# Frequency 32 as a member of frequency 0's group: four groups a block instead of five, in a fused convolution and spectral-filter kernel

## The chip, the cores and the metric

The kernel runs on one core of a Trainium2 chip. A core has a matrix engine (PE, its weight loads shown as PEld), a vector engine (DVE), an activation engine (ACT), GpSimd (POOL) and a queue engine (SP). SP, ACT and POOL also issue transfers, which sixteen DMA engines carry out. The metric is the device time of one execution in microseconds (us); what is compared is the median of several runs. The profile is one execution with its own span.

## The reference, cut to what matters

```python
x = A_u                                            # (1, 2048, 640)
g = sigmoid((x * gate_w).sum(-1, keepdims=True))
# a: long convolution over time, one kernel K[d, l] per channel, by FFT of length 4096
y = irfft(rfft(x^T, 4096) * rfft(K, 4096), 4096)[:, :, :2048]
a = y^T + x * D_skip
# b: 2-D real FFT over time and channel, times a complex weight, and back
b = irfft2(rfft2(x) * (w_r + 1j * w_i), s=(2048, 640))
out = g * a + (1 - g) * b
```

The kernel K is itself computed (`K = 2 Re sum_n C exp(A dt l)`). Only the convolution's inverse and the last sum are touched by the change.

## The kernel before, in words

The 640 channels are worked on in four blocks of 160 (`c` = 0 to 3). A transform of length 4096 is split in two: 33 outer frequencies k = 0 to 32, each with an inner transform of 64 points as a matrix product with a table of its own (`T.w2` forward, `T.w3` back), and an outer real transform of 32 points (tables `T.e1` forward; `T.e3`, `T.e3e` back). `POS_K` orders the frequencies: first the sixteen odd ones, then the even ones 0, 2, ... 32, so frequency 0 stands at place `K0` = 16 and frequency 32 at place 32, alone behind two sets of sixteen. A frequency has a real and an imaginary outer part, 64 rows each. Frequencies 0 and 32 are real on the outer side, so each of them needs only one half of such a pair.

Earlier phases make the transforms of the input (`u_d` in DRAM), the filtered half b (`s3e_d`) and the kernel K (`k_d`). The change lies in `phase_d` alone, the last stage, about 177 us long. For each block it does, in groups of four pairs of frequencies:

- `load`: fetch the group's part of `u_d` into the tile `us` (L782, issued on ACT's queue).
- `fronts`: PE multiplies by `w2` (helper line L348, tile `p_s`); DVE and POOL form the complex product with `us` (L795, L796, L800, L801) into `t2`. Two pairs make one half of a group.
- `backs`: PE multiplies `t2` by `w3` (L814, tile `p_i`); ACT copies the result into `s3` (L816; two buffers) and stores it in `s3_d` (L823), 640 KB a group. `backs` of a group runs behind the `fronts` of a later one: the list `late` holds two groups back, near the end one.

Beside this main stream, `merge` mixes in three others by weights written by hand:

- `first`: the forward outer transform of the next block's K (L335 with ACT copies L336), ten pieces a block.
- `last_e(c, a)`: the outer inverse of half b, in two calls a block (L160, tile `p_e`, then DVE L875 into `oe`).
- `last_c(c, a)`: the outer inverse of the convolution of block c, in two calls (L892, tile `p_c`, DVE L897, then a sum with `oe`, and the store of `out`). It reads the tile `t3`, which `load_c` fetches from `s3_d` on SP's queue in two loads of 1280 KB (L865), each when the stores of its rows have landed.

Frequency 32 is a fifth group of its own: half a pair on 64 partitions, with two matmuls in `fronts` and two in `backs`, a copy of 128x160 (L818) and a store of 40 KB (L820) to row 33 of `s3_d`. Row 33 is the row of frequency 0's unused half, which group 8's store has written before, so L820 waits on ACT until that store has landed.

A block thus has five steps g (for c = 3 the small group comes fourth). `last_e(c)` runs at g = 1 and 2 (for c = 0 at 2 and 3); `load_c(c-1)` at g = 1 and 2; `last_c(c-1)` at g = 3 and 4 for c = 1 and 2. For c = 3, `load_c(3)` begins at g = 2 and 3, and both calls of `last_c(2)` stand behind the last group, before `last_c(3)`. What stands in each engine's program is a static order that the framework derives from the code's order, tile buffers and its own estimate of times; each engine takes its instructions in that order.

Of the kernel before, what the change touches and what calls it, by code (L numbers as in the profile page):

```python
# [765 lines left out]
def phase_d(tc, A, T, ctx, out):  # L766
    nc = tc.nc
# [16 lines left out]
    def fronts(c, g0, gn, st):  # L784
        nl, us = st.nl, st.us
        nj = nl // 64

        t2 = st.t2 = wk.tile([128, 8, 160], F32, tag="t2", name="t2")
        for h in range(0, gn, 2):
            hn = min(2, gn - h)  # L790
            pv, _ = stage2(nc, ps, T.w2, T.t1[c], g0 + h, hn)
            uu = us[:nl, h:h + hn]
            ma = wk.tile([128, 2, 2, 160], F32, tag="ma", name="ma")
            mb = wk.tile([128, 2, 2, 160], F32, tag="mb", name="mb")
            V.tensor_tensor(out=ma[:nl, :hn], in0=pv, in1=uu, op=ALU.mult)  # L795
            V.tensor_tensor(out=mb[:nl, :hn], in0=pv, in1=uu[:, :, ::-1, :], op=ALU.mult)  # L796
            for j in range(nj):
                l = slice(64 * j, 64 * j + 64)
                o = slice(nj * h + j, nj * (h + hn), nj)
                (G if j else V).tensor_tensor(out=t2[0:64, o, :], in0=ma[l, :hn, 0, :], in1=ma[l, :hn, 1, :], op=ALU.subtract)  # L800
                (V if j else G).tensor_tensor(out=t2[64:128, o, :], in0=mb[l, :hn, 0, :], in1=mb[l, :hn, 1, :], op=ALU.add)  # L801
            yield 0.55 * hn

    def backs(c, g0, gn, st):
        t2 = st.t2
        s3 = w2k.tile([128, 8 if gn > 1 else 1, 160], F32, tag="s3%d" % min(2, gn), name="s3")
        np_ = gn * st.nl // 64
        k0 = 2 * g0
        for h in range(0, np_, 4):
            hn = min(4, np_ - h)  # L810
            p = ps.tile([128, 2, 512], F32, tag="ps", name="p_i2")
            for i in range(hn):
                for x in (0, 64):
                    T.mm = P.matmul(p[x:x + 64, i // 2, 160 * (i % 2):160 * (i % 2) + 160], T.w3[:, k0 + h + i, x:x + 64], t2[:, h + i, :], start=True, stop=True)  # L814
            if hn == 4:
                S.copy(s3[:, h:h + 4, :].rearrange("p (x y) d -> p x (y d)", x=2), p[:, :, 0:320])  # L816
            else:
                S.copy(s3[:, h, :], p[:, 0, 0:160])  # L818
            if k0 == 32:
                nc.scalar.dma_start(T.s3_d[c, 33], s3[0:64, 0, :])  # L820
            elif h or (c, g0) == (3, 12):
                x = h if (c, g0) == (3, 12) else 0
                T.sd = nc.scalar.dma_start(T.s3_d[c, 2 * (k0 + x):2 * (k0 + h) + 8].rearrange("(x k) a d -> (k a) x d", k=2), s3[:, x:h + 4, :])  # L823
            yield 0.27 * hn

    groups = [(c, g0, min(4, 17 - g0)) for c in range(4) for g0 in ((0, 4, 8, 12, 16), (0, 4, 8, 16, 12))[c == 3]]
    late, sts, t3s, t3es, oes = [], {}, {}, {}, {}

    def mains(i):
# [7 lines left out]
        while len(late) > (1 if i > 15 else 2):  # L837
# [111 lines left out]
    run(last_c(2, 0))  # L949
# [27 lines left out]
```

## Time and profile before

| | |
|---|---|
| runs | 617.16 us median of 3 (616.8 to 620.78) |
| profiled execution | 616.28 us, of which span 614.5 us |
| last stage | from about 437.8 us to the end of the span |
| DMA in the whole span | 101.98 MB |
| small stores (L820) | 4, 40 KB each |
| copies of 128x160 on ACT (L818) | 4, 0.29 us each |

How to read it: the timeline lists instructions by start and busy time, with the idle time of the engine ahead of them in brackets and what ended it. In the timeline and the chain an fp32 matmul shows as two records, so x16 is eight matmuls. "issue" means that the profile shows nothing that the engine waited for; a wait for a transfer can hide there. A stage's table gives each engine's busy time, the clock granted to PE and the busy share of the DMA engines.

### The profile page before, as it was taken

The numbers are of one execution on the slowest core, as the hardware profiler recorded it, in microseconds if no ns is written. First come the engines' busy times: TensorE is split into PE (matmuls) and PEld (weight loads), VectorE is DVE, ScalarE is ACT, GpSimd is POOL, SyncE is SP. The second block draws the span as 40 slices with busy tenths as digits, with TensorE's granted clock in tenths as the row PEclk, the third lists the DMA queues.
The fourth block names the chain that finished last, engine by engine and source line by source line (L and its number), as shares of the span: only waits on it lengthen the run. The fifth ranks groups of instructions, "written<-read, shape, count | busy, mean of one in ns | idle before, by whom it ended". The sixth has DMA issues, their size and how long they took to land.

```text
span 614.5 us, 16646 instructions
## 1 busy us (share of the span) xinstructions
PE 539.0 (88%) x7084; PEld 411.1 (67%) x7084; DVE 500.0 (81%) x748; ACT 364.6 (59%) x659; POOL 267.2 (43%) x246
## 2 busy tenths in 40 slices
PE   9688989989968989989799989898989979998864
PEld 6576667766746666766667766566878768787731
DVE  6961697598899988999999999978496975987863
ACT  4556675677847777897599897798523213231210
POOL 4921261152527344455326334345243546565450
PEclk9899989989979987999799999999989989999987
DMA  8787204154512411243242122115967989799985
GB/s 340 304 290 248 70 25 167 30 200 153 215 44 65 138 44 54 66 137 109 65 139 69 36 87 89 49 45 183 349 228 264 259 264 325 230 298 288 260 217 195
DMA packets 47987, 101.98 MB, mean 166 GB/s; under 512 B 3220, under 2 KB 32680, under 8 KB 46152
## 3 DMA queue, kind: packets, MB, share of 16 engines
q1 hardware_dynamic: 24792, 67.74, 34.0%
q10 hardware_dynamic: 20080, 22.52, 11.8%
q0 software_dynamic: 3040, 10.65, 5.3%
q8 instruction: 56, 0.92, 0.6%
q14 instruction: 19, 0.16, 0.1%
HBM read 60.91 MB, written 39.98 MB: 164 GB/s over the span
## 4 chain that ended last, share of the span: by engine, by line
PE 49%; DVE 26%; DMA 9%; ACT 9%; issue 4%; POOL 1%; ACTq 0%; SPq 0%; DVEq 0%; POOLq 0%
PE p_eo L551 8%; PE p_s L335 7%; PE p_s L348 7%; PE p_e L638 5%; PE p_k L693 4%; DMA s_d<-s 3%; PE p_i L814 3%; DVE q L652 2%; PE p_c L892 2%; PE p_p L649 2%; PE p_d L518 2%; PE p_i L565 2%; PE p_t L502 2%; DVE ma L795 2%; PE p_d L519 2%
## 5 line engine op out<-in xcount | busy, mean ns | idle before, releaser
L679 POOL TENSOR_TENSOR y<-e,sc 128x512 f32<-128x512 f32 x40 | 56.7, 1417 | 131.3 <-ACT sc L665 71.9
L348 PE MATMUL p_s<-t,w 128*64 128x160 f32 x1056 | 94.4, 317 | 10.3 <-ACT ut L382 4.5
L348 PEld LDWEIGHTS p_s<-t,w 128*64 128x64 f32 x1056 | 78.0, 140 | 21.2 <-ACT ut L382 5.4
L640 ACT ACTIVATE e<-p_e 128x512 f32<-128x512 f32 x120 | 68.6, 601 | 22.8 <-PE p_e L638 20.4
L551 PE MATMUL p_eo<-td,pmt 107*128 107x321 f32 x204 | 69.0, 458 | 3.9 <-ACT pmt L505 3.9
L693 PE MATMUL p_k<-x,y 128*32 128x64 f32 x2560 | 63.7, 229 | 9.9 <-DVE x L677 2.9
L693 PEld LDWEIGHTS p_k<-x,y 128*32 128x32 f32 x2560 | 46.1, 113 | 38.2 <-issue 29.4
L336 ACT COPY t<-p_s 128x512 f32<-128x512 f32 x40 | 24.5, 621 | 74.0 <-PE p_s L335 54.1
L652 DVE SCALAR_TENSOR_TENSOR q<-q,p_p 128x512 f32<-128x512 f32 x80 | 53.4, 681 | 13.5 <-ACT q L651 11.7
L638 PE MATMUL p_e<-rm,par 128*128 128x512 f32 x120 | 58.8, 520 | 3.4 <-ACT e L640 2.8
L680 POOL TENSOR_TENSOR y<-e,sc 128x512 f32<-128x512 f32 x40 | 54.4, 1359 | 6.5 <-ACT sc L666 6.5
L800 POOL TENSOR_TENSOR t<-ma 64x320 f32<-64x320 f32 x32 | 28.3, 883 | 60.5 <-DVE ma L795 50.8
L551 PEld LDWEIGHTS p_eo<-td,pmt 107*128 107x128 f32 x204 | 38.4, 198 | 19.5 <-ACT pmt L505 6.9
L677 DVE TENSOR_TENSOR x<-e,cx 128x1024 f32<-128x1024 f32 x40 | 48.5, 1213 | 2.2 <-ACT cx L668 2.2
L651 ACT ACTIVATE q<-p_p 128x512 f32<-128x512 f32 x80 | 46.5, 592 | 4.3 <-PE p_p L649 3.8
L335 PEld LDWEIGHTS p_s<-c,kt 128*64 128x64 f32 x640 | 41.2, 141 | 11.5 <-issue 6.7
L335 PE MATMUL p_s<-c,kt 128*64 128x128 f32 x640 | 45.2, 281 | 3.9 <-DVE mb L796 2.0
L814 PE MATMUL p_i<-t,w 128*64 128x160 f32 x528 | 45.0, 305 | 3.6 <-POOL t L801 2.8
L649 PE MATMUL p_p<-rp,par 128*128 128x512 f32 x80 | 43.3, 547 | 4.5 <-DVE q L652 4.4
L795 DVE TENSOR_TENSOR ma<-p_s,us 128x640 f32<-128x640 f32 (+1 forms) x36 | 28.2, 783 | 19.9 <-PE p_s L348 12.5
L814 PEld LDWEIGHTS p_i<-t,w 128*64 128x64 f32 x528 | 38.8, 139 | 8.0 <-POOL t L801 3.4
L816 ACT COPY s<-p_i 128x640 f32<-128x640 f32 x32 | 21.8, 693 | 37.6 <-PE p_i L814 28.5
(153 smaller groups left out, 1190.6 us busy)
## 6 DMA issues: line engine op xcount, KB each, us to landing
u_d<-ut SPq DMA_DIRECT2D x32, 320.0 KB, 2.7
us<-u_d ACTq DMA_DIRECT2D x16, 640.0 KB, 6.4
s_d<-s ACTq DMA_DIRECT2D x15, 640.0 KB, 8.6
t<-s_d SPq DMA_DIRECT2D x6, 1280.0 KB, 10.0
ww<-in_w_l SPq DMA_DIRECT2D x8, 642.0 KB, 4.0
ue<-u_d SPq DMA_DIRECT2D x8, 640.0 KB, 4.4
k_d<-kt SPq DMA_DIRECT2D x4, 1280.0 KB, 7.7
kt<-k_d SPq DMA_DIRECT2D x8, 640.0 KB, 9.2
```

Of the source, the lines that this page charges most:

```text
L335: nc.tensor.matmul(p[64 * ri:64 * ri + 64, j, :], src(i + j), e1[ri], start=True, stop=True)
L348: ins = nc.tensor.matmul(p[64 * j:64 * j + 64, i, 160 * ri:160 * ri + 160], w2[:, x, 64 * ri:64 * ri + 64], t1[:, x // 2 if x < 32 else K0 ...
L551: P.matmul(p[:, :E], st.pmt[:DC, c, w, j, :], tv[:DC, w, c, :], start=c == 0, stop=c == 2)
L638: P.matmul(p[:, :], pars[t], rm[:, c:c + 512], start=True, stop=True)
L640: st.exp = S.activation(ef[:, c:c + 512], p[:, :], AF.Exp)
L649: P.matmul(p[:, :], pars[t], rp[:, c:c + 512], start=True, stop=True)
L652: V.scalar_tensor_tensor(out=qf[:, c:c + 512], in0=qf[:, c:c + 512], scalar=MAGIC, in1=p[:, :], op0=ALU.subtract, op1=ALU.subtract)
L677: V.tensor_tensor(out=x[:, 0].rearrange("p d (h j) -> p d h j", h=2), in0=e[:, :, 0:64].rearrange("p d (h j) -> p d h j", h=2), in1=cx.uns ...
L679: G.tensor_tensor(out=y[:, 1], in0=e[:, :, 64:96], in1=sc[:, 0], op=ALU.mult)
L680: G.tensor_tensor(out=y[:, 0], in0=e[:, :, 64:96], in1=sc[:, 1], op=ALU.mult)
L693: P.matmul(st.pb[32 * r:32 * r + 32, o, :], y[:, ri, 4 * qq + JR[r], :], x[:, ri, 4 * qq + JR[r], :], start=t % 2 + qq + 1 - ri == 0, stop ...
L814: T.mm = P.matmul(p[x:x + 64, i // 2, 160 * (i % 2):160 * (i % 2) + 160], T.w3[:, k0 + h + i, x:x + 64], t2[:, h + i, :], start=True, stop ...
```

## The change

Frequency 32 joins the group that begins at pair 8, the group of frequency 0. In `fronts` that group has a third, smaller part, with its own small tile `u1` and transfer. `t2` has nine columns, and the ninth holds frequency 32. In `backs`, the 64-row matmul that would compute the unused half of frequency 0 takes frequency 32's table and column instead, so its result lands in the right row of the same PSUM bank and goes out with the group's copy and store. A block has four groups; the fifth group's matmuls in `backs`, its copy and its store are gone. The other streams are placed anew: `last_e` at g = 1 and 2 in every block, `last_c(c-1, 0)` at g = 3, `last_c(c-2, 8)` at g = 0 of the block after, `last_c(2, 0)` at g = 3 of the last block, three pieces of `first` a step instead of two, and `late` shrinks to one from step 13.

```diff
-    def load(c, g0, gn, st):
-        nl = st.nl = 128 if g0 < 16 else 64
+    def load(c, g0, st):
         st.us = up.tile([128, 4, 2, 160], F32, tag="us", name="us")
-        nc.scalar.dma_start(st.us[:nl, 0:gn], T.u_d[c, :nl, g0:g0 + gn])
+        nc.scalar.dma_start(st.us[:, :], T.u_d[c, :, g0:g0 + 4])
+        if g0 == 8:
+            st.u1 = w2k.tile([64, 1, 2, 160], F32, tag="u1", name="u1")
+            nc.scalar.dma_start(st.u1[:, :], T.u_d[c, 0:64, 16:17])
...
-        t2 = st.t2 = wk.tile([128, 8, 160], F32, tag="t2", name="t2")
-        for h in range(0, gn, 2):
-            hn = min(2, gn - h)
-            pv, _ = stage2(nc, ps, T.w2, T.t1[c], g0 + h, hn)
-            uu = us[:nl, h:h + hn]
+        t2 = st.t2 = wk.tile([128, 9, 160], F32, tag="t2", name="t2")
+        for h in (0, 2, 4)[:3 if g0 == 8 else 2]:
+            hn, nl = (2, 128) if h < 4 else (1, 64)
+            nj = nl // 64
+            pv, _ = stage2(nc, ps, T.w2, T.t1[c], g0 + h if h < 4 else 16, hn)
+            uu = st.us[:, h:h + 2] if h < 4 else st.u1
...
-        for h in range(0, np_, 4):
-            hn = min(4, np_ - h)
+        for h in (0, 4):
             p = ps.tile([128, 2, 512], F32, tag="ps", name="p_i2")
-            for i in range(hn):
+            for i in range(4):
                 for x in (0, 64):
-                    T.mm = P.matmul(p[x:x + 64, i // 2, 160 * (i % 2):160 * (i % 2) + 160], T.w3[:, k0 + h + i, x:x + 64], t2[:, h + i, :], start=True, stop=True)
-            if hn == 4:
-                S.copy(s3[:, h:h + 4, :].rearrange("p (x y) d -> p x (y d)", x=2), p[:, :, 0:320])
-            else:
-                S.copy(s3[:, h, :], p[:, 0, 0:160])
-            if k0 == 32:
-                nc.scalar.dma_start(T.s3_d[c, 33], s3[0:64, 0, :])
-            elif h or (c, g0) == (3, 12):
+
+                    k, y, o = (32, 0, 8) if x and k0 + h + i == K0 else (k0 + h + i, x, h + i)
+                    T.mm = P.matmul(p[x:x + 64, i // 2, 160 * (i % 2):160 * (i % 2) + 160], T.w3[:, k, y:y + 64], t2[:, o, :], start=True, stop=True)
+            S.copy(s3[:, h:h + 4, :].rearrange("p (x y) d -> p x (y d)", x=2), p[:, :, 0:320])
+            if h or (c, g0) == (3, 12):
...
-    groups = [(c, g0, min(4, 17 - g0)) for c in range(4) for g0 in ((0, 4, 8, 12, 16), (0, 4, 8, 16, 12))[c == 3]]
+    groups = [(c, g0) for c in range(4) for g0 in (0, 4, 8, 12)]
...
-        while len(late) > (1 if i > 15 else 2):
+        while len(late) > (1 if i > 12 else 2):
...
-        for g in range(5):
+        for g in range(4):
             beside = []
-            if g - (c == 0) in (1, 2):
-                beside = [last_e(c, AG * (g - 1 - (c == 0)))]
-            if c and g == 1:
-                load_c(c - 1, 0, 32)
-            if c and g == 2:
-                load_c(c - 1, 32, 32)
-            if c in (1, 2) and g > 2:
-                beside += [last_c(c - 1, AG * (g - 3))]
-            if g == 4 and c < 3:
+            if g in (1, 2):
+                beside = [last_e(c, AG * (g - 1))]
+            if c and g in (1, 2):
+                load_c(c - 1, 32 * (g - 1), 32)
+            if c and g == 3:
+                beside = [last_c(c - 1, 0)]
+            if c > 1 and g == 0:
+                beside = [last_c(c - 2, AG)]
+            if g == 3 and c < 3:
                 load_e(c + 1)
-            if c == 3 and g in (2, 3):
+            if c == 3 and g > 1:
                 load_c(3, 16 * (g - 2), 16)
...
-            streams = [(4.8, mains(5 * c + g))]
+            streams = [(4.8, mains(4 * c + g))]
...
-                streams.append((2.1, some(fst, 2 if g < 4 else 9)))
+                streams.append((2.1, some(fst, 3 if g < 3 else 9)))
...
     load_c(3, 48, 16, 2)
-    run(last_c(2, 0))
     run(last_c(2, AG))
```

Three places of the engines' order, before and changed. The first is PE in block 1, at the end of the step g = 1 (`p_s` with `kt` is a piece of `first`). Before:

```order
L335 MATMUL p_s_6089<-c_65,kt 64x128 x7
L814 MATMUL p_i_6100<-t_5897,w_5268 64x160 [waits Activation_49,Pool_49]
L814 MATMUL p_i_6100<-t_5897,w_5268 64x160
L160 MATMUL p_e<-t3e,c_65 64x320 [waits DVE_49]
L160 MATMUL p_e<-t3e,c_65 64x320
```

Changed:

```order
L335 MATMUL p_s_6078<-c_65,kt 64x128 x7
L815 MATMUL p_i_6089<-t_5859,w_5268 64x160 [waits Activation_49,Pool_49]
L815 MATMUL p_i_6089<-t_5859,w_5268 64x160 x7
L160 MATMUL p_e<-t3e,c_65 64x320 [waits DVE_49]
L160 MATMUL p_e<-t3e,c_65 64x320
L815 MATMUL p_i_6103<-t_5859,w_5268 64x160 [waits DVE_49,PE_49]
L815 MATMUL p_i_6103<-t_5859,w_5268 64x160 x7
```

Before, the two matmuls of `backs(0, 16)` stand here, and `backs(0, 12)` stood at g = 0; now the sixteen of `backs(0, 12)` stand here.

The second is the end of PE's program. Before, `backs(3, 12)` ends, and then both calls of `last_c(2)` follow (`t_6854` is block 2's `t3`):

```order
L814 MATMUL p_i_7097<-t_7044,w_5268 64x160 [waits DVE_49]
L814 MATMUL p_i_7097<-t_7044,w_5268 64x160 x5
L892 MATMUL p_c<-t_6854,c_65 64x480 [waits DMAHW7_49,DMAHW5_49]
L892 MATMUL p_c<-t_6854,c_65 64x480 x3
L892 MATMUL p_c<-t_6854,c_65 64x320 [waits DVE_49]
```

Changed (`p_i_7062` is `backs(3, 8)`, `p_i_7074` and `p_i_7085` are `backs(3, 12)`, `t_6817` is block 2's `t3`):

```order
L815 MATMUL p_i_7062<-t_6920,w_5268 64x160 [waits DVE_49,PE_49]
L815 MATMUL p_i_7062<-t_6920,w_5268 64x160 x2
L888 MATMUL p_c<-t_6817,c_65 64x480 [waits DMAHW6_49,DMAHW3_49]
L888 MATMUL p_c<-t_6817,c_65 64x480 x3
L815 MATMUL p_i_7062<-t_6920,w_5268 64x160 x2
L888 MATMUL p_c<-t_6817,c_65 64x320 [waits DVE_49]
L888 MATMUL p_c<-t_6817,c_65 64x320
L815 MATMUL p_i_7062<-t_6920,w_5268 64x160 x3
L815 MATMUL p_i_7074<-t_7000,w_5268 64x160 [waits Activation_49,Pool_49]
L815 MATMUL p_i_7074<-t_7000,w_5268 64x160 x7
L815 MATMUL p_i_7085<-t_7000,w_5268 64x160 [waits DVE_49,Pool_49]
```

`last_c(2, 0)` with its wait for two loads now stands ahead of all of `backs(3, 12)`. On DVE its first product likewise stands ahead of the last two products of `fronts(3, 12)`, where nothing stood before:

```order
L796 TENSOR_TENSOR ma<-p_s_7024,us 128x640 [waits PE_49,Pool_49]
L797 TENSOR_TENSOR mb<-p_s_7024,us 128x640 [waits Pool_49]
L893 TENSOR_TENSOR ot<-p_c,gate 128x480 [waits DMASW5_49,PE_49]
L801 TENSOR_TENSOR t_7000<-ma 64x2x160 [waits DVE_49]
L802 TENSOR_TENSOR t_7000<-mb 64x2x160 [waits DVE_49]
```

The third is the end of ACT's program. Before:

```order
L816 COPY s_7085<-p_i_7086 128x640 [waits DMAHW0_49,PE_49]
L820 DMA s_d<-s_7079 64x160 [waits DMAHW1_49,Activation_49]
L823 DMA s_d<-s_7085 128x4x160 [waits DMAHW4_49,Activation_49]
L816 COPY s_7085<-p_i_7097 128x640 [waits PE_49]
L823 DMA s_d<-s_7085 128x4x160 [waits DMAHW5_49,Activation_49]
```

Changed:

```order
L816 COPY s_7073<-p_i_7074 128x640 [waits DMAHW4_49,PE_49]
L816 COPY s_7073<-p_i_7085 128x640 [waits PE_49]
L819 DMA s_d<-s_7073 128x4x160 [waits Activation_49] x2
```

The small store with its wait is gone, and both halves of the last group's store now follow the second copy.

More of the change, by code (lines that the diff above doesn't have):

```diff
@@ L777, in phase_d, with fronts @@
     pd = ctx.enter_context(tc.tile_pool(name="d_ps", reuse_waits="tile", bufs=2, space=PSUM))
-    def load(c, g0, gn, st):
-        nl = st.nl = 128 if g0 < 16 else 64
+    def load(c, g0, st):
         st.us = up.tile([128, 4, 2, 160], F32, tag="us", name="us")
-        nc.scalar.dma_start(st.us[:nl, 0:gn], T.u_d[c, :nl, g0:g0 + gn])
-    def fronts(c, g0, gn, st):
-        nl, us = st.nl, st.us
-        nj = nl // 64
-        t2 = st.t2 = wk.tile([128, 8, 160], F32, tag="t2", name="t2")
-        for h in range(0, gn, 2):
-            hn = min(2, gn - h)
-            pv, _ = stage2(nc, ps, T.w2, T.t1[c], g0 + h, hn)
-            uu = us[:nl, h:h + hn]
+        nc.scalar.dma_start(st.us[:, :], T.u_d[c, :, g0:g0 + 4])
+        if g0 == 8:
+            st.u1 = w2k.tile([64, 1, 2, 160], F32, tag="u1", name="u1")
+            nc.scalar.dma_start(st.u1[:, :], T.u_d[c, 0:64, 16:17])
+    def fronts(c, g0, st):
+        t2 = st.t2 = wk.tile([128, 9, 160], F32, tag="t2", name="t2")
[4 more added lines that the diff above has]
+            uu = st.us[:, h:h + 2] if h < 4 else st.u1
             ma = wk.tile([128, 2, 2, 160], F32, tag="ma", name="ma")
             mb = wk.tile([128, 2, 2, 160], F32, tag="mb", name="mb")
-            V.tensor_tensor(out=ma[:nl, :hn], in0=pv, in1=uu, op=ALU.mult)
+            V.tensor_tensor(out=ma[:nl, :hn], in0=pv, in1=uu[:, :], op=ALU.mult)
             V.tensor_tensor(out=mb[:nl, :hn], in0=pv, in1=uu[:, :, ::-1, :], op=ALU.mult)
```

9 lines of the change are left out of this document (4 added, 5 removed).

## The prediction

> **What bounds the kernel now.** I read the page first, for the span, and then a table of the last stage cut at the starts of its blocks, since the change lies there alone.
>
> ```profile
> span 614.5 us, 16646 instructions
> ```
>
> ```profile
> core 0: us, PE busy (x) PEld busy (x) DVE busy (x) ACT busy (x) POOL busy (x), PEclk, DMA share, GB/s
> 437.80:472.30 34.50, 31.80 (x412) 28.53 (x412) 29.36 (x41) 10.73 (x17) 15.47 (x17) 0.95 0.75 270
> 472.30:516.50 44.20, 38.64 (x472) 32.80 (x472) 32.80 (x47) 11.74 (x19) 22.05 (x23) 0.96 0.93 278
> 516.50:556.10 39.60, 36.90 (x472) 31.41 (x472) 33.28 (x48) 11.76 (x19) 23.43 (x25) 1.00 0.93 277
> 556.10:590.70 34.60, 28.27 (x324) 22.89 (x326) 29.60 (x42) 6.67 (x11) 16.86 (x19) 0.97 1.01 273
> 590.70:614.50 23.80, 13.00 (x50) 3.70 (x48) 9.58 (x23) 0.69 (x1) 5.73 (x5) 0.79 0.64 195
> ```
>
> Blocks 0, 1 and 2 are PE's: it is busy 31.80 of 34.50, 38.64 of 44.20 and 36.90 of 39.60 us. In block 3 PE has 6 us free and DVE, busy 29.60 of 34.60, sets the pace. The DMA engines are busy throughout, so a transfer lands long after its issue. The fifth row is the tail: store, load, `last_c(3)`, output.
>
> I then read PE's timeline for the block boundaries and its waits.
>
> ```profile
> 472.35 1.36 PE L348 MATMUL p_s<-t,w 128*64 128x160 f32 x16 [0.69 <-ACT t L336]
> 485.85 1.36 PE L348 MATMUL p_s<-t,w 128*64 128x160 f32 x16 [0.51 <-DVE mb L796]
> 502.36 1.63 PE L892 MATMUL p_c<-t,c 128*64 128x480 f32 x5 [3.70 <-issue]
> 516.53 1.35 PE L348 MATMUL p_s<-t,w 128*64 128x160 f32 x16 [0.46 <-ACT t L336]
> 529.96 1.35 PE L348 MATMUL p_s<-t,w 128*64 128x160 f32 x16 [0.47 <-DVE mb L796]
> 543.67 1.39 PE L892 MATMUL p_c<-t,c 128*64 128x480 f32 x5 [0.91 <-DVE t L800]
> ```
>
> The rows at 502.36 and 543.67 are `last_c`, which waits 3.70 us in block 1 and 0.91 in block 2. The first wait is a load; the transfers show it:
>
> ```profile
> 492.27 0.45 SPq L865 DMA_DIRECT2D t<-s_d  x1
> ```
>
> ```profile
> t<-s_d SPq DMA_DIRECT2D x1, 1280.0 KB, 10.0
> t<-s_d SPq DMA_DIRECT2D x1, 1280.0 KB, 9.1
> t<-s_d SPq DMA_DIRECT2D x1, 1280.0 KB, 11.0
> ```
>
> These are the second loads of `t3` issued at 492.27, 534.46 and 571.12. The first lands at 492.27 + 10.0 = 502.3, when `last_c` starts. So stores and loads matter where `last_c` waits for them in PE's order.
>
> **The change part by part.** First the unit prices, from the chain of waits inside block 2, where PE runs without a pause, and from DVE's part of that chain in block 3:
>
> ```profile
> 534.10 1.14 PE p_s L348 x16
> 535.24 0.81 PE p_e L160 x4
> 536.04 0.87 PE p_s L335 x16
> 536.92 1.09 PE p_i L814 x16
> 538.00 0.54 PE p_e L160 x4
> ...
> 552.25 0.92 PE p_c L892 x4
> ...
> 564.06 0.82 DVE ma L795
> 564.89 0.73 DVE mb L796
> 565.62 0.56 DVE t L800
> 566.20 1.05 DVE t L801
> 567.28 0.66 DVE oe L875
> ```
>
> On PE, half a group's `fronts` cost 1.14, a piece of `first` 0.87, half a group's `backs` 1.09 (with its small gap 1.15, so 2.3 a group), and a call of `last_e` or `last_c` two parts of 0.8 to 0.9 and one of 0.54: I take 2.4. Two matmuls of `backs` cost 2/8 of 1.09, 0.27. On DVE half a group is 0.82 + 0.73 + 0.56 + 1.05 and a gap, 3.2, and a call of `last_e` or `last_c` three parts of up to 0.66, 1.9.
>
> Block 0. `backs(0, 8)` moves to block 1: -2.3. The tenth piece of `first` no longer stands last, so most of the 0.69 us that PE waits for its copy at 472.35 goes: -0.4. `last_e(0)` now stands one front earlier and waits for its table's load: two more pieces and one front fewer stand ahead of it, at most +1.1, at least 0; I take +0.5. Sum -2.2.
>
> Block 1. It gives `backs(1, 8)` away and gets `backs(0, 8)`: nothing. The call `last_c(0, 8)` leaves: -2.4. The two matmuls go: -0.27. The pauses around the small group (0.51 at 485.85) and at the block's end (0.46 at 516.53) go: -0.95. Then the wait of `last_c(0, 0)`. The store of group 12, on which its second load hangs, moves from g = 0 to g = 1. By the unit prices g = 0 is 2.3 + 3 x 0.87 + 2.3 = 7.2, g = 1 is 2.4 more, 9.6, g = 2 is 9.9 with frequency 32, and up to `last_c` in g = 3 there is 1.14 + 0.87, 2.1. With 1.5 us of pauses `last_c` is reached 30.3 us into the block. The store is issued at 7.2 + 9.6 less the last piece, plus pause and copy, 1.6: 17.5. How long it takes to land is the disputed price.
>
> ```profile
> s_d<-s ACTq DMA_DIRECT2D x15, 640.0 KB, 8.6
> ```
>
> ```profile
> s_d<-s ACTq DMA_DIRECT2D x1, 640.0 KB, 4.1
> ...
> s_d<-s ACTq DMA_DIRECT2D x1, 640.0 KB, 11.5
> ```
>
> The median of 15 such stores is 8.6; the one at 459.47, with little else under way, takes 4.1, and the one at 480.37, behind the first load of `t3`, 11.5. In the changed block that load is issued some 5 us in and has landed by 15, before the store, so I take 6.5, between 4.1 and 8.6, and 9.5 for the load (rows of 9.1 to 11.0). It lands at 17.5 + 6.5 + 9.5 = 33.5, and `last_c` waits 3.2 instead of 3.7: -0.5. Sum of block 1: -2.4 - 0.27 - 0.95 - 0.5 = -4.1.
>
> Block 2. `last_c(0, 8)` comes in and `last_c(1, 8)` leaves: nothing. The two matmuls go (-0.27) and two pauses (0.47 at 529.96 and one like 0.46): -0.9. All of g = 0 is 2.4 longer, so the store goes out at 19.9, the load lands at 35.9, and `last_c(1, 0)` is reached at 32.7: a wait of 3.2 where 0.91 stood, +2.3. A wait of that size also costs clock:
>
> ```profile
> 502.30:506.50 4.20, 4.14 (x26) 3.28 (x28) 2.97 (x5) 0.00 (x0) 2.13 (x2) 0.63 1.05 432
> 448.00:452.00 4.00, 4.00 (x45) 4.00 (x42) 3.94 (x5) 0.62 (x1) 2.44 (x3) 0.60 0.65 264
> ```
>
> After the 3.70 us wait PE is granted 0.63 over 4.2 us, a loss of 1.6; and the second row, behind a wait of under 2 us, has 0.60. So I add 1.6 for a wait of 3.2. The Trainium skill, "TensorE: Matmul & The Clock Gate", section "What's actually happening", has the clock halved only after an idle window of about 3.4 us; by that page a wait of 3.2 may go free, and the sum would be 1.6 lower. The row after the shorter wait speaks against it, and the sum keeps the 1.6. Sum of block 2: -0.27 - 0.9 + 2.3 + 1.6 = +2.7.
>
> Block 3. It gets `backs(2, 8)` (2.3 on PE), `last_c(1, 8)` at g = 0 and `last_c(2, 0)` at g = 3 (2.4 each on PE, 1.9 each on DVE). In the tail `last_c(2, 0)` had cost nothing: PE waited for the last load there anyway. PE would hold 28.27 + 7.1 = 35.4, DVE 29.60 + 3.8 = 33.4 and its 1.5 us start, both about the length of the block. DVE alone sets the least: its last product came 32.8 into the block and comes 1.9 + 0.66 later, then half of `backs`, 36.5 against 34.6, so +1.9. More is set by the load that `last_c(2, 0)` waits for. `backs(2, 12)` ends 14.9 into the block (DVE needs 1.5 + 6.5 + 1.9 for g = 0 and then half of g = 1); the store lands 8 later, since the first load of `t3` still runs beside it; the load takes 11.0, as it did in this block before: 33.9. From there 1.1 of `p_c`, 0.66 on DVE, 1.7 for the last two products and 1.2 of `backs` end PE's work at 38.6 instead of 34.6. Queued behind that wait are all of `backs(3, 12)` on PE and the last two products on DVE, and for these the last store, the last load and the end. +4.0.
>
> Tail. Before, the small store held up the last copy:
>
> ```profile
> 590.79 0.48 ACTq L820 DMA_DIRECT2D s_d<-s  x1
> 591.37 0.55 ACTq L823 DMA_DIRECT2D s_d<-s  x1
> 591.96 0.69 ACT L816 COPY s<-p_i 128x640 f32<-128x640 f32 x1 [4.42 <-PE p_i L814]
> 592.68 0.37 ACTq L823 DMA_DIRECT2D s_d<-s  x1
> ```
>
> PE had ended at 590.7 and the last store left at 592.68, 2.0 later. Without L820 it is copy and two issues, 1.2 to 1.3: -0.7. The first half now leaves with the second, so the store may land later; at worst that takes all of the 0.7 back.
>
> Other edits cost nothing: `u1` is the same 80 KB on the same queue; DVE's and POOL's small products are the same, in another place; 0.29 us of copy a block on ACT, busy 11.74 of 44.20, is free either way; 40 KB a block, at 277 GB/s, is 0.14 us of the DMA engines, hidden unless they set the pace.
>
> Sum: -2.2 - 4.1 + 2.7 + 4.0 - 0.7 = -0.3. The profiled execution took 616.28 (span and 1.8 around it), so 616.0; the median of the runs, 617.16, is 0.9 above that execution. Within 1% of that median, 611.0 to 623.3, is about what a measurement of this kernel can tell from no change.
>
> **The rivals.** First, the loads are in time. If stores land as the one at 459.47 did (4.1) and loads in 9.1, `last_c` waits 0.4 in blocks 1 and 2, the lost clock of both goes, and block 3 has only DVE's +1.9. Block 1 is then -2.4 - 0.27 - 0.95 - 3.3 - 1.6 = -8.5, block 2 -0.27 - 0.9 - 0.5 = -1.7: -2.2 - 8.5 - 1.7 + 1.9 - 0.7 = -11.2, 605.1. For it: the first load has landed before the store. Against it: only one of the rows above has such a store. The Trainium skill, "DMA: Bandwidth & Descriptors", section "Anatomy of one DMA — SWDGE (gpsimd) path", gives 2.0 us plus the bytes at 436 GB/s, which would be an estimate of 3.5 for the store and 5.0 for the load, and this rival would hold; the trace's 10.0 and 11.0 speak against it.
>
> Second, slower: group 12's store becomes the kernel's longest wait. If it takes 11.5 and the load 11.0, `last_c` waits 9.7 in blocks 1 and 2 and block 3's load comes at 37.4. Block 1 is -3.6 + 6.0 = +2.4, block 2 +8.8 + 1.6 - 1.2 = +9.2, block 3 37.4 + 4.7 + 1.6 - 34.6 = +9.1: 17.8 in all, 634.1. The time passes 623.3 when each of the three chains is 2.4 later than I take it, so from 18.4 us for store and load together. For it: the median store is 8.6 and these engines are busy over 0.9. Against it: the long stores lay beside a load of `t3`, and here that mostly comes earlier.
>
> Third, the change does little of what it says, since the DMA engines set the pace: their share is 0.93 in blocks 1 and 2 and 1.01 in block 3. Then work moved between PE and DVE changes nothing, the bytes saved are worth 4 x 0.14 and the tail 0.7: 615.0. Against it: the share drops to 0.75 in block 0, and in blocks 1 and 2 PE's own work fills the time.
>
> **How the numbers follow.** The forecast, 616.0, has a chance of 0.45; the first rival 0.22, the second 0.18, the third 0.15. The forecast and the third lie within 1%; a few hundredths of the forecast's reach below 611.0 make up for what the first rival's smaller forms leave above it, so faster is 0.22, and slower 0.18. The forecast's own range, from block 0's and the tail's ends and one us a load, is 612 to 620. The range that should hold 8 in 10 reaches most of the way to the first rival and a part of the way to the second: 606.5 to 624.
>
> **What would show it.** Right: no L820; in blocks 1 and 2 `last_c` waits about 3 us with a low clock behind it; block 0 some 2 shorter, block 1 some 4 shorter, block 2 and block 3 longer by some 3 and 4; in the last step PE idle ahead of `p_c`, and DVE's last products behind it. Wrong: no wait ahead of `p_c` (first rival), waits over 6 us (second), or blocks whose length does not move (third).

## The result, and the profile after

The changed kernel took 630.87 us, the median of 6 runs (625.62 to 632.32); on the same chip the kernel before took 616.98 (6 runs). The ratio is 1.025, with a 95% interval of 1.0215 to 1.0293: slower, and outside the predicted range of 606.5 to 624. The same kernel run later beside the one before gave 625.93 against 619.58, a ratio of 1.015 (1.0055 to 1.0252). Some executions fall into a slower state, and all ratios here and below leave those out, so that they need not be the quotients of the medians beside them. The kernel was slower both times; by how much varies, and the second interval begins at half a per cent.

The profiled execution took 631.36 us. The table of the last stage, cut at the starts of its blocks on PE as in the prediction:

```profile
span 629.6 us, 16612 instructions
```

```profile
core 0: us, PE busy (x) PEld busy (x) DVE busy (x) ACT busy (x) POOL busy (x), PEclk, DMA share, GB/s
442.10:476.50 34.40, 28.95 (x380) 24.62 (x381) 28.27 (x40) 8.77 (x15) 14.41 (x16) 1.00 0.77 284
476.50:522.10 45.60, 37.05 (x455) 30.96 (x456) 32.05 (x45) 11.47 (x18) 17.75 (x20) 0.93 0.86 245
522.10:564.00 41.90, 36.67 (x472) 32.60 (x470) 32.78 (x47) 11.53 (x18) 23.43 (x25) 1.00 0.85 249
564.00:603.70 39.70, 34.65 (x380) 28.28 (x378) 34.78 (x50) 7.52 (x11) 23.24 (x26) 0.96 0.87 235
603.70:629.60 25.90, 9.80 (x37) 2.89 (x33) 8.33 (x20) 1.29 (x2) 3.96 (x4) 0.72 0.76 223
```

Block 1 has given away PE work, 37.05 us busy where it had 38.64, and is longer. Block 3 has PE busy 34.65 where it was 28.27. From here on all kernels are compared by one measure: a block runs from its first product `ma` on DVE to the next block's, block 3 to the end of the last `p_i` on PE, the tail from there to the span's end. In us:

| kernel | starts at | block 0 | block 1 | block 2 | block 3 | tail | sum |
|---|---|---|---|---|---|---|---|
| before | 439.2 | 34.6 | 44.2 | 39.6 | 33.4 | 23.5 | 175.3 |
| changed | 443.6 | 34.5 | 45.7 | 42.0 | 38.1 | 25.9 | 186.0 |
| changed, second profile (`again`, below) | 437.8 | 34.7 | 44.1 | 44.4 | 37.4 | 25.0 | 185.6 |

So the stage became 10.3 to 10.7 us longer. The other 4.4 us of the first profile lie ahead of the stage, where nothing was changed; the second profile doesn't have them.

PE's timeline of the changed kernel shows the waits (the bracket is the idle time before the row, and what ended it):

```profile
457.57 2.62 PE L160 MATMUL p_e<-t3e,c 128*64 128x480 f32 x12 [1.82 <-DMA t3e<-s3e_d]
476.51 1.37 PE L348 MATMUL p_s<-t,w 128*64 128x160 f32 x16 [0.84 <-DVE mb L797]
503.40 1.31 PE L815 MATMUL p_i<-t,w 128*64 128x160 f32 x16 [1.27 <-DVE mb L797]
514.50 1.87 PE L888 MATMUL p_c<-t,c 128*64 128x480 f32 x4 [6.67 <-DMA t<-s_d]
558.80 1.03 PE L888 MATMUL p_c<-t,c 128*64 128x480 f32 x4 [3.38 <-DMA t<-s_d]
586.50 1.42 PE L348 MATMUL p_s<-t,w 128*64 128x160 f32 x16 [3.28 <-ACT s L816]
597.87 1.03 PE L888 MATMUL p_c<-t,c 128*64 128x480 f32 x4 [0.33 <-DMA t<-s_d]
```

`last_c` waits 6.67 us in block 1 (3.70 before) and 3.38 in block 2 (0.91 before). The third `last_c` of this kind, `last_c(2, 0)` in block 3 at 597.87, waits almost nothing. In its place PE stops at 586.50 for a copy of ACT. The transfers behind the first two waits, from the timelines of SP and ACT:

```profile
483.59 0.46 SPq L861 DMA_DIRECT2D t<-s_d  x1
493.44 0.38 ACTq L819 DMA_DIRECT2D s_d<-s  x1
501.48 0.45 SPq L861 DMA_DIRECT2D t<-s_d  x1
502.17 0.39 SPq L850 DMA_DIRECT2D t3e<-s3e_d  x1
541.05 0.38 ACTq L819 DMA_DIRECT2D s_d<-s  x1
548.03 0.44 SPq L861 DMA_DIRECT2D t<-s_d  x1
```

In block 1 group 12's store is issued at 493.44, 15.4 us into the block; the load that hangs on it follows at 501.48, 8.0 later; `last_c` starts when it lands, at 514.50, 13.0 after that, beside a table load of the same size issued 0.7 behind it. In block 2 the store takes 7.0 and the load 10.8.

Each long wait may cost clock as well. The windows of 4.2 us behind three of these rows (last columns: granted clock, DMA share, GB/s):

```profile
558.80:563.00 4.20, 4.20 (x43) 3.38 (x45) 2.58 (x4) 0.00 (x0) 2.08 (x3) 1.00 0.93 332
514.50:518.70 4.20, 4.20 (x21) 2.74 (x23) 0.74 (x2) 0.00 (x0) 1.20 (x1) 0.50 0.91 332
587.70:591.90 4.20, 4.20 (x31) 2.92 (x27) 3.81 (x6) 0.00 (x0) 1.86 (x2) 0.60 1.10 290
```

Behind the 6.67 us wait PE does 21 matmuls in 4.2 us instead of 43. Behind the 3.38 us wait no clock is lost; behind the 3.28 us wait at 586.50 it is.

ACT's timeline shows what PE waited for in block 3, and the tail:

```profile
571.88 0.38 ACTq L819 DMA_DIRECT2D s_d<-s  x1
585.76 1.29 ACT L816 COPY s<-p_i 128x640 f32<-128x640 f32 x2 [5.92 <-DMA s_d<-s]
602.31 0.37 ACTq L819 DMA_DIRECT2D s_d<-s  x1
606.61 2.74 ACTq L861 DMA_DIRECT2D t<-s_d  x1
```

The store issued at 571.88 lands 13.8 us later, beside a 1280 KB load of `t3` issued 1.9 ahead of it; ACT has two `s3` buffers, and its copy at 585.76 waits 5.92 us for that store. In the tail the chain of waits goes through the store of group 8 at 602.31 and a load whose issue alone took 2.74 us, where the same issue at 593.29 took 0.35 before:

```profile
602.31 3.89 DMA s_d<-s
...
606.61 8.61 DMA t<-s_d
```

### The profile page after: what moved, and what is told of

Read it like the earlier page. It is cut to its first block, busy times and chain, and to the rows that moved or that the text cites. A ratio compares the mean times of both kernels' runs of the same rounds, so it can differ in the third digit from the quotient of the medians.

```text
span 629.6 us, 16612 instructions
## 1 busy us (share of the span) xinstructions
PE 540.3 (86%) x7068; PEld 413.0 (66%) x7068; DVE 501.9 (80%) x748; ACT 363.8 (58%) x655; POOL 266.6 (42%) x246
## 3 DMA queue, kind: packets, MB, share of 16 engines
q1 hardware_dynamic: 24792, 67.74, 33.8%
q10 hardware_dynamic: 19760, 22.35, 11.5%
## 4 chain that ended last, share of the span: by engine, by line
PE 40%; DVE 25%; DMA 20%; ACT 9%; issue 3%; POOL 1%; SPq 0%; ACTq 0%; DVEq 0%; POOLq 0%
PE p_eo L551 8%; DMA t<-s_d 7%; PE p_s L348 5%; PE p_e L638 5%; DMA s_d<-s 5%; PE p_k L693 3%; DVE q L652 3%; PE p_s L335 3%; PE p_c L888 3%; PE p_i L565 2%; PE p_t L502 2%; DVE x L677 2%; PE p_p L649 2%; DVE aq L662 2%; PE p_i L815 2%
## 5 line engine op out<-in xcount | busy, mean ns | idle before, releaser
L348 PE MATMUL p_s<-t,w 128*64 128x160 f32 x1056 | 98.4, 318 | 10.8 <-ACT ut L382 5.3
L348 PEld LDWEIGHTS p_s<-t,w 128*64 128x64 f32 x1056 | 81.3, 142 | 23.2 <-ACT ut L382 5.9
L551 PE MATMUL p_eo<-td,pmt 107*128 107x321 f32 x204 | 70.3, 465 | 3.9 <-ACT pmt L505 3.8
L693 PE MATMUL p_k<-x,y 128*32 128x64 f32 x2560 | 61.8, 225 | 9.6 <-DVE x L677 2.6
L693 PEld LDWEIGHTS p_k<-x,y 128*32 128x32 f32 x2560 | 44.7, 111 | 37.1 <-issue 29.0
L652 DVE SCALAR_TENSOR_TENSOR q<-q,p_p 128x512 f32<-128x512 f32 x80 | 53.1, 680 | 12.8 <-ACT q L651 11.0
L796 DVE TENSOR_TENSOR ma<-p_s,us 128x640 f32<-128x640 f32 x32 | 26.3, 822 | 28.1 <-PE p_s L348 13.5
L649 PE MATMUL p_p<-rp,par 128*128 128x512 f32 x80 | 44.4, 560 | 4.6 <-DVE q L652 4.4
L335 PE MATMUL p_s<-c,kt 128*64 128x128 f32 x640 | 43.6, 274 | 3.9 <-DMA kt<-k_d 1.8
L335 PEld LDWEIGHTS p_s<-c,kt 128*64 128x64 f32 x640 | 39.6, 137 | 10.2 <-issue 2.5
L888 PE MATMUL p_c<-t,c 128*64 128x480 f32 (+1 forms) x96 | 27.8, 619 | 21.5 <-issue 10.5
```

The costliest lines, as they stand in the source:

```text
L335: nc.tensor.matmul(p[64 * ri:64 * ri + 64, j, :], src(i + j), e1[ri], start=True, stop=True)
L348: ins = nc.tensor.matmul(p[64 * j:64 * j + 64, i, 160 * ri:160 * ri + 160], w2[:, x, 64 * ri:64 * ri + 64], t1[:, x // 2 if x < 32 else K0 ...
L551: P.matmul(p[:, :E], st.pmt[:DC, c, w, j, :], tv[:DC, w, c, :], start=c == 0, stop=c == 2)
L649: P.matmul(p[:, :], pars[t], rp[:, c:c + 512], start=True, stop=True)
L652: V.scalar_tensor_tensor(out=qf[:, c:c + 512], in0=qf[:, c:c + 512], scalar=MAGIC, in1=p[:, :], op0=ALU.subtract, op1=ALU.subtract)
L693: P.matmul(st.pb[32 * r:32 * r + 32, o, :], y[:, ri, 4 * qq + JR[r], :], x[:, ri, 4 * qq + JR[r], :], start=t % 2 + qq + 1 - ri == 0, stop ...
```

## The experiments

All edits are made to the changed kernel. Six theories stand in the expectations. **A**: the late store of group 12, and with it `t3`'s second load, makes `last_c` wait. **B**: block 3 is held by the two `s3` buffers and their stores. **C**: that frequency 32 shares the group and the bank costs in itself. **D**: the prediction's step for block 3, `last_c(2, 0)` waiting there for its load ahead of the last group. **E**: the new places of `last_e` and `last_c` cost. **F**: the longer list of late groups costs whichever group is late. Each ratio is to the kernel before, run beside it on the same chip, so ratios may be compared; medians were taken on several chips and compare less well. Each stage length is of one profiled execution. The stage table of all of them:

| kernel | block 0 | block 1 | block 2 | block 3 | tail | sum |
|---|---|---|---|---|---|---|
| late1 | 37.8 | 36.6 | 38.5 | 37.7 | 22.5 | 173.2 |
| tail | 34.5 | 45.7 | 41.5 | 34.2 | 27.4 | 183.3 |
| s3x3 | 34.2 | 44.1 | 41.9 | 39.0 | 24.1 | 183.3 |
| five | 33.9 | 45.3 | 39.5 | 33.8 | 24.9 | 177.4 |
| early12 | 34.6 | 37.6 | 40.1 | 39.4 | 25.1 | 176.9 |
| only12late | 37.7 | 37.1 | 39.3 | 36.6 | 22.8 | 173.5 |
| blk3 | 34.6 | 43.4 | 43.4 | 42.0 | 23.1 | 186.4 |
| late1tail | 37.8 | 36.6 | 38.5 | 32.6 | 24.6 | 170.0 |
| late1tail_e0 | 35.3 | 39.9 | 38.3 | 32.7 | 25.9 | 172.2 |
| all3 | 38.9 | 36.6 | 41.9 | 32.3 | 24.8 | 174.5 |

**late1: one late group instead of two.**

```diff
-        while len(late) > (1 if i > 12 else 2):
+        while len(late) > 1:
```

> The changed kernel with one number changed: the backward step of a group always runs one group behind, so group 12's store leaves at step 0 of the next block again, as in the kernel before. Theory A (the late store of group 12 makes last_c wait): the waits of 6.7 us in block 1 and 3.4 in block 2 fall below 1 us, the low clock behind the first goes, blocks 1 and 2 together lose 8 to 11 us; time 620 to 623. Theory B (block 3 and its s3 buffers are the cost): blocks 1 and 2 lose no more than 3, block 3 stays near 39.7; time 628 or more. Theory C (frequency 32's place in the group costs by itself): no change, 630.

Measured: 614.58 us, ratio 1.001 (0.9973 to 1.0045). This one line takes back the whole loss. PE's and SP's timelines:

```profile
505.26 1.00 PE L888 MATMUL p_c<-t,c 128*64 128x480 f32 x4
544.20 1.03 PE L888 MATMUL p_c<-t,c 128*64 128x480 f32 x4 [0.39 <-DMA t<-s_d]
579.07 1.07 PE L888 MATMUL p_c<-t,c 128*64 128x480 f32 x2 [3.15 <-DVE t L801]
492.54 0.44 SPq L861 DMA_DIRECT2D t<-s_d  x1
```

```profile
437.80:475.70 37.90, 31.13 (x418) 27.01 (x416) 28.76 (x40) 10.11 (x17) 14.76 (x17) 1.00 0.77 281
475.70:512.00 36.30, 34.44 (x460) 29.67 (x458) 30.73 (x43) 11.29 (x19) 16.67 (x18) 1.00 1.00 287
```

The second load is issued at 492.54, 15.7 us into block 1. It takes 11.5, within the 9.3 to 13.3 of the other kernels, and lands at 504.0, before `last_c` is reached at 505.26. Block 1 runs at full clock and takes 36.6 instead of 45.7; block 0 is 3.3 longer: one group's `backs` (2.3 on PE) is now in it, and PE waits 2.88 there for the table's load instead of 1.82. A holds for blocks 1 and 2, which lose 12.6 together, more than the 8 to 11 that A expected, and the time is below its 620 to 623. Block 3 stays long, and `last_c(2, 0)` there now waits 3.15 us for DVE, not for a load.

**tail: `last_c(2, 0)` back behind the last group.**

```diff
-            if c and g == 3:
+            if c in (1, 2) and g == 3:
...
+    run(last_c(2, 0))
     run(last_c(2, AG))
```

> The changed kernel with last_c(2, 0) put back behind the last group, where the kernel before had it. Theory A: blocks 1 and 2 unchanged; block 3 gains the 2 us of DVE work that leaves it, the tail has room for it: 628 to 629. Theory D (the prediction's step for block 3: last_c(2, 0)'s wait for its load holds up the last group): 4 us or more, 626 or less. Theory B: the wait for the s3 buffer stays at about 6 us and the gain is under 1: 630.

Measured: 630.68 us, ratio 1.031 (1.0222 to 1.0395); its stage began 445.5 us into the span. Inside the stage, block 3 is 34.2 instead of 38.1 and the tail 27.4 instead of 25.9. ACT's wait for a buffer is still there:

```profile
586.47 1.29 ACT L816 COPY s<-p_i 128x640 f32<-128x640 f32 x2 [5.09 <-DMA s_d<-s]
```

So it is `last_c(2, 0)`, not the buffer, that lengthens block 3 by about 4 us; the tail takes back 1.5 of it. The time of the whole doesn't show a gain: it fits B's 630 and misses D's 626, so D is borne out by the length of block 3 alone. Block 1, where nothing was changed against the changed kernel, again has the long wait of `last_c` (6.74 us, for a load that took 13.3).

**s3x3: three `s3` buffers.**

```diff
-        s3 = w2k.tile([128, 8, 160], F32, tag="s3", name="s3")
+        s3 = w3k.tile([128, 8, 160], F32, tag="s3", name="s3")
...
-        t2 = st.t2 = wk.tile([128, 9, 160], F32, tag="t2", name="t2")
+        t2 = st.t2 = wk.tile([128, 8, 160], F32, tag="t2", name="t2")
+        tx = st.tx = w1k.tile([128, 1, 160], F32, tag="tx", name="tx") if g0 == 8 else None
```

Here `w3k` has three buffers, and for want of room frequency 32's column and `u1` have a single one.

> The changed kernel with three s3 buffers instead of two (frequency 32's column and small tile get single buffers of their own, to make room). Theory B: the 5.9 us that ACT waits in block 3 for the store of group 8 of block 2 go, PE's 3.3 us wait and the low clock behind it go, block 3 loses 4 us: 626 to 627. Theory A: block 3 loses at most 2, since DVE is as long as the block, and blocks 1 and 2 stay: 629 or more.

Measured: 624.56 us, ratio 1.018 (1.0132 to 1.0231). ACT waits for no buffer any more, but block 3 is 39.0, not shorter:

```profile
592.36 1.25 PE L892 MATMUL p_c<-t,c 128*64 128x480 f32 x4 [3.64 <-DMA t<-s_d]
```

The wait for the buffer has made room for the wait for the load that the prediction had put there. B is a cause of the wait that one sees, not of the block's length: two causes end at nearly the same time, and taking one away shows the other. The time, 624.56, is below what either theory expected (626 to 627, or 629 and more); block 1 is 44.1 here, as in the second profile of the changed kernel.

**five: frequency 32 joined, the old placement in five steps.** Step 4 has no group; `last_e`, `last_c` and the loads stand as they stood before.

```diff
-        for g in range(4):
+        for g in range(5):
...
-            streams = [(4.8, mains(4 * c + g))]
+            streams = [(4.8, mains(4 * c + g))] if g < 4 else []
```

> Frequency 32 joins the group, but the other streams keep the places of the kernel before: five steps, the fifth without a group. Theory A: group 12's store still leaves at step 1 of the next block, so last_c still waits 3 to 7 us in blocks 1 and 2; time 625 to 630. Theory E (the new places of last_e and last_c are the cost, not the store): back to the kernel before, 616 to 619. Theory C: 630.

Measured: 619.41 us, ratio 1.010 (1.0049 to 1.0158).

```profile
506.91 1.87 PE L888 MATMUL p_c<-t,c 128*64 128x480 f32 x4 [5.04 <-DMA t<-s_d]
547.20 1.83 PE L888 MATMUL p_c<-t,c 128*64 128x480 f32 x8 [0.60 <-DMA t<-s_d]
```

Blocks 2 and 3 are as before the change; block 1 keeps a wait of 5.04, since the list of late groups is still two long and group 12's store goes out 14.2 us into the block. The joining itself (C) leaves no more than about 1%, and part of that is A's. A's time, 625 to 630, missed, and E's, 616 to 619, came nearly true: with the old places the same late list makes the stage 2.1 us longer than before the change, and not 10.3 to 10.7. So the late store costs little without the new places of the other streams. In block 3 it is `last_c(2, 0)`'s place that matters (tail); in block 2, 2.5 shorter here, the places were not tried one by one.

**early12: group 12 alone is taken out of the list early.**

```diff
-        while len(late) > (1 if i > 12 else 2):
+        while len(late) > (1 if i > 12 or i in (4, 8) else 2):
```

> The changed kernel with only group 12's backward step brought forward: at step 0 of blocks 1 and 2 the list of late groups is emptied to one, so groups 8 and 12 of the block before both go there; block 3 is untouched. Theory A (the wait of last_c for group 12's store and load): the waits of 6.7 and 3.4 us and the low clock go, the last stage falls from 186.0 to 175 to 178, block 3 keeps about 38; time 619 to 622. Theory F (a deeper list of late groups costs in every block, whatever group it is): no more than half of that, 625 or more.

Measured: 619.74 us, ratio 1.008 (1.0035 to 1.0123).

```profile
508.98 1.03 PE L888 MATMUL p_c<-t,c 128*64 128x480 f32 x4 [0.43 <-DMA t<-s_d]
```

The store leaves 9.0 us into block 1, the wait is 0.43, and blocks 1 and 2 together are 10.0 us shorter than in the changed kernel's profile. With every other group still late, this is A and not F, in this kernel.

**only12late: group 12 alone stays late.**

```diff
-        while len(late) > (1 if i > 12 else 2):
+        while len(late) > (2 if i in (4, 8) else 1):
```

> The kernel with the short list of late groups, with only group 12's backward step put one step later in blocks 1 and 2. Theory A: the waits of last_c come back, 6 and 3 us with a low clock, the last stage grows from 173.2 by 8 to 12; time 622 to 626. Theory F: within 2 us of the short list, 613 to 617.

Measured: 617.70 us, ratio 1.004 (0.998 to 1.009). A's 622 to 626 missed, and the stage, 173.5 against late1's 173.2, is what F expected. So A's simple form, in which the step of group 12's `backs` decides, doesn't hold:

```profile
498.58 0.45 SPq L861 DMA_DIRECT2D t<-s_d  x1
507.92 1.03 PE L888 MATMUL p_c<-t,c 128*64 128x480 f32 x4 [1.09 <-DMA t<-s_d]
```

Group 12's store still leaves late, 13.6 us into block 1. But with group 8's store out of the way the first load of `t3` goes 1.5 us into the block instead of 5.6, the second 20.0 instead of 23.5, and the wait is 1.09. What decides is when the second load is issued and how long it takes, and the issue is set by the whole row of stores and loads ahead of it: a late group 12 costs when the groups ahead of it are late too.

**blk3: block 3 with one late group from its first step on.**

```diff
-        while len(late) > (1 if i > 12 else 2):
+        while len(late) > (1 if i > 11 else 2):
```

> The changed kernel with the list emptied to one already at step 0 of block 3, so groups 8 and 12 of block 2 both go there. Theory B (in block 3 the store of group 8 lies beside the first load of t3, holds an s3 buffer for 13.8 us and with it ACT, PE and the clock): block 3 falls from 38.1 to 34 to 36, blocks 1 and 2 keep their waits; 626 to 628. If the work moved into block 3 is the cost and not the order of its stores, block 3 stays at 38: 630.

Measured: 628.95 us, ratio 1.019 (1.0093 to 1.0291). Block 3 is 42.0, longer than in the changed kernel; the tail is 23.1. B's expectation missed, but the edit didn't take away the wait that B names. With the stores of groups 8 and 12 close together, ACT stands idle for 11.72 us ahead of a copy, until a store has freed a buffer, where it was 5.92:

```profile
581.62 1.29 ACT L816 COPY s<-p_i 128x640 f32<-128x640 f32 x2 [11.72 <-DMA s_d<-s]
```

So this run is no test of B. Why the block grew further was not followed up.

**late1tail: late1 and tail together.** Its edit is those two diffs.

> The short list of late groups, and last_c(2, 0) back behind the last group. PE waits 8.2 us there for the last load, so the call is free in the tail, while in block 3 it stands in a chain that DVE sets: 2 us less than with the short list alone, 612 to 613, and so about 2 us under the kernel before. If block 3's length is set by its stores, no change, 614 to 615.

Measured: 613.89 us, ratio 0.995 (0.9901 to 0.9993).

```profile
550.70:584.30 33.60, 28.20 (x330) 22.61 (x328) 32.08 (x47) 6.84 (x10) 22.48 (x25) 1.00 0.98 272
```

Block 3 is 32.6, 5.1 less than in late1; the tail gives 2.1 back. In this block DVE is busy 32.08 of 33.60: it sets the pace, and `last_c(2, 0)`'s products are better behind the last group's. The ratio can't be told from late1's; the gain is in the profile.

**again: the changed kernel once more.**

> The changed kernel once more, nothing altered, to see which parts of its profiled execution repeat. Its last stage began 443.6 us into the span, 4.4 us later than the 439.2 of the kernel before, though nothing ahead of the stage was changed. If that is chance in one execution, the stage now begins 438 to 442 us in, or anywhere up to 445, and the stage itself is again 184 to 187 us long, with last_c's waits of 6 to 7 us in block 1 and about 3 in block 2. If the change itself delays the beginning, it is again at 443 to 445. Time about 630 by both.

Measured: 625.93 us, ratio 1.015 (1.0055 to 1.0252). The stage began at 437.8, so the 4.4 us ahead of it in the first profile don't belong to the change; its length repeats, 185.6. The waits of 6 to 7 us in block 1 and the time of about 630 that were expected did not repeat. PE's timeline, and the window behind its second row:

```profile
506.88 1.87 PE L888 MATMUL p_c<-t,c 128*64 128x480 f32 x4 [4.62 <-DMA t<-s_d]
551.29 1.86 PE L888 MATMUL p_c<-t,c 128*64 128x480 f32 x4 [3.13 <-DMA t<-s_d]
581.27 1.07 PE L348 MATMUL p_s<-t,w 128*64 128x160 f32 x6 [2.35 <-ACT s L816]
```

```profile
551.30:555.50 4.20, 4.20 (x21) 2.73 (x23) 0.76 (x2) 0.00 (x0) 1.20 (x1) 0.50 0.98 356
```

The load of block 1 took 11.0 here, and the wait is 4.62 instead of 6.67. In block 2 the wait is 3.13, less than the 3.38 of the first profile, yet here the clock halves, and the block is 44.4 instead of 42.0.

**late1tail_e0: block 0's `last_e(0)` one step later.**

```diff
-            if g in (1, 2):
-                beside = [last_e(c, AG * (g - 1))]
+            if g - (c == 0) in (1, 2):
+                beside = [last_e(c, AG * (g - 1 - (c == 0)))]
```

> late1tail with block 0's last_e(0) back at g = 2 and 3, as before the change (in late1tail PE waits 2.8 us there for its table's load t3e, at 452.99, and block 0 is 37.8 long, where it was 34.6). Theory A2, that block 0's length comes from that wait: block 0 is 34.5 to 35.5 and the time 611 to 612. Rival, that block 0 is held by the group that the shorter list of late groups puts into it (backs(0, 8), 2.3 on PE, which block 1 no longer has) and by DVE: the wait goes but block 0 stays at 37 to 38, and the time stays at 613 to 614.

Measured: 612.55 us, ratio 0.994 (0.9891 to 0.998). PE's timeline of late1tail, and of this kernel:

```profile
452.99 1.03 PE L160 MATMUL p_e<-t3e,c 128*64 128x480 f32 x4 [2.81 <-DMA t3e<-s3e_d]
```

```profile
454.92 0.62 PE L160 MATMUL p_e<-t3e,c 128*64 128x480 f32 x1 [1.68 <-DMA t3e<-s3e_d]
487.81 1.03 PE L160 MATMUL p_e<-t3e,c 128*64 128x480 f32 x4 [2.62 <-DMA t3e<-s3e_d]
```

Block 0 is 35.3 as expected, with a wait of 1.68 instead of 2.81. But the buffer of `t3e` comes free later, block 1's table load is issued 32.5 us into block 0 instead of 26.6, and block 1 waits 2.62 us for it. The two blocks together are 75.2 instead of 74.4: the wait has moved on. The time can't be told from late1tail's.

**all3: late1tail with three `s3` buffers.**

> late1tail with three s3 buffers (and frequency 32's column of t2 in a tile of its own). Theory B, that a wait of ACT for an s3 buffer still holds up stores in block 3: its wait goes and block 3 or the tail is 1 to 2 us shorter, 612. Rival: with group 12's store early, block 3 is DVE's and the tail is store and load; no gain, 613.5 to 614.5.

Measured: 612.20 us, ratio 0.990 (0.9862 to 0.994), the lowest ratio of all; its interval overlaps those of late1tail and late1tail_e0. In late1tail ACT waits for a buffer once at the end of block 3, and in all3 that wait is gone:

```profile
583.70 1.48 ACT L816 COPY s<-p_i 128x640 f32<-128x640 f32 x2 [2.96 <-DMA s_d<-s]
```

But the second half of that copy has to wait for PE, whose last `p_i` ends at 584.4 in late1tail, so that the wait hid behind PE; block 3 is 32.3 against 32.6. The stage of its profile is longer (174.5), in blocks 0 and 2, where nothing was meant to change. Whether the third buffer gains anything is open.

## Why the prediction was wrong

The terms of the prediction's sum, beside what the two profiles of the changed kernel show against the kernel before:

| term | predicted | first profile | second profile |
|---|---|---|---|
| block 0 | -2.2 | -0.1 | +0.1 |
| block 1 | -4.1 | +1.5 | -0.1 |
| block 2 | +2.7 | +2.4 | +4.8 |
| block 3 | +4.0 | +4.7 | +4.0 |
| tail | -0.7 | +2.4 | +1.5 |
| sum | -0.3 | +10.7 (of rounded terms 10.9) | +10.3 |

**Block 1 failed first, and by most.** Its mechanism was right: `last_c` waits for the load that hangs on group 12's store. The step that failed is the term for that load's landing. The prediction counts from PE's first product of the block, 476.51 in the first profile and 470.94 in the second; so counted, in us:

| step in block 1 | predicted | first profile | second profile |
|---|---|---|---|
| store issued | 17.5 | 16.9 | 16.9 |
| store takes | 6.5 | 8.0 | 8.0 |
| load issued | 24.0 | 25.0 | 24.9 |
| load takes | 9.5 | 13.0 | 11.0 |
| `last_c` reached | 30.3 | 31.3 | 31.3 |
| `last_c` waits | 3.2 | 6.67 | 4.62 |

The load is issued 1.0 late and `last_c` is reached 1.0 late, which cancel; what is left, 3.5 and 1.5, is the load. Why it takes so long isn't shown. A table load of the same size goes out 0.7 behind it here, but in five, with one 0.5 behind, it took 10.9, and in late1, with one 8.4 behind, 11.5. With the wait goes the clock, which the prediction counted as lost alike before and after: granted 0.50 behind the wait now, 0.63 before. And the 0.95 us of pauses that were to go came back in other places, such as the 1.27 at 503.40. late1, with no wait and a clock of 1.00, has a block 1 of 36.6; the prediction's block without its wait and clock, 44.2 - 4.1 - 3.2 - 1.6, was 35.3. The difference, 1.3, is left for these pauses; most of the rest is wait and clock.

**Block 0 gained nothing.** The wait of `last_e(0)` was bounded at 1.1 and taken as 0.5; it is 1.82 and 2.00. The bound counted the pieces that no longer stand ahead of it on PE. In fact PE reaches it 1.7 us earlier in the block than before, 12.2 where it was 13.9. The load lands later besides, 14.0 and 14.2 us into the block where it was 13.3; its issue moved from 0.4 to 3.2 and 2.1, which the bound left out. Nor did the pause at the block's end go, 0.84 us at 476.51 where 0.69 stood; it is now for DVE instead of a copy.

**Block 2 was right**, within what the two profiles leave: a wait of 3.38 or 3.13 where 3.2 was forecast. Some of this is luck: store and load took 17.8 and 17.4 us together where 16.0 was taken, but in the first profile the store left about 1 us early, 541.05 less 522.10 into the block where 19.9 was taken. The 1.6 us of lost clock is absent in the first profile and there in the second, so the +2.4 of the first agrees with the forecast for another reason than the one given.

**Block 3 was right in size by luck, and its wait was another.** The prediction had `last_c(2, 0)` stand waiting for its load; in fact it waits 0.33, because the groups ahead of it are already late, held by ACT's wait for a buffer, and DVE is loaded to 34.78 of 39.70. s3x3 shows the predicted wait underneath (3.64), tail shows that `last_c(2, 0)`'s place costs 3.9, and late1 that with neither of these waits it still costs: there PE waits 3.15 for DVE.

**The tail failed in sign.** No small store holds up the last copy any more, and in late1 the tail is 1.0 shorter than before. But in the changed kernel the issue of ACT's last load takes 2.74 us, and it lands 8.61 after the issue began, where it took 6.0 before. In the second profile the issue takes 2.64. Why it takes so long isn't shown, and it doesn't go with the list of late groups: it is 0.33 to 0.35 in nine of the other kernels, with the long list and the short one, and 3.23 in all3, which has the short one. In tail and late1tail it is the stores just ahead of it that take long to issue, 3.56 and, for two, 3.98:

```profile
605.16 3.56 ACTq L819 DMA_DIRECT2D s_d<-s  x1
```

Nor is it all of the tail's loss: in early12, with an issue of 0.34, the tail is 25.1.

**The whole.** The sum of -0.3 was wrong by 10.6 to 11 us: block 1 missed by 4.0 to 5.6, block 0 and the tail by 2.1 to 3.1 each. late1 and early12 show that the loss, or most of it, goes when group 12's `backs` stands a step earlier; five and only12late show that its late step alone is not enough. Nearly all of the loss needs the late list and the new places of the other streams together.

The first rival falls: in block 1 store and load took 8.0 and 11.0 to 13.0 us, and in block 2 about 7 and 10.5 to 10.8, where it had 4.1 and 9.1. The second rival named the direction and the place, store and load together over 18.4 us: they took 21.0 and 19.0 in block 1. Its size was too large, since in block 2 they took 17.8. The third rival falls: between the changed kernel and late1 the bytes are the same, and the stage differs by 12.8 us.

What stays open: why the load of block 1 takes 11 to 13 us; the issue of 2.74 us; the longer block 3 of blk3; and why the same kernel's stage can begin anywhere from 437.8 to 445.5 us in these profiles.

## What to carry to other kernels

When work is put off by one more step, follow the stores that it ends in to the loads that hang on them and to the first instruction that waits there, and where the DMA engines are busy price the chain by the longest rows of its kind as well as by the middle ones. A pause of about 3 us on PE should be priced both with and without the lost clock, and the range be made to hold both. Where two waits end at about the same time, taking away the one that the profile names shows only the other: take away both before judging either.

## What the runs showed of the hardware

The clock did not go by the length of the wait alone. Waits of 3.13, 3.28 and 6.67 us were followed by a granted clock of 0.50, 0.60 and 0.50 over some 4 us, a wait of 3.38 by 1.00. In blk3 a wait of the same 3.38 us, at the same place, was followed by 0.59:

```profile
553.10:557.30 4.20, 4.20 (x23) 2.96 (x25) 1.40 (x3) 0.00 (x0) 1.20 (x1) 0.59 0.96 350
```

The Trainium skill, "TensorE: Matmul & The Clock Gate", section "What's actually happening", has an idle window of about 3.4 us that runs free of the program. A window with a phase of its own agrees with waits of nearly one length that differ in outcome; that a wait of 3.13 us was enough does not agree with the figure as a threshold on the wait.

A store of 640 KB took 3.89 us to land in the tail, 8.0 in block 1 and 13.8 in block 3 right behind a load; the second load of `t3` in block 1, 1280 KB, took from 9.3 (only12late, 498.58 to 507.92) to 13.3 (tail, 503.18 to 516.52). The issue of the same load on ACT's queue took 0.34 us in one kernel and 2.74 in another.
